# An attention and feed-forward kernel: the input weights kept resident in float32, their state product made plainly by row halves

## The chip, the cores and the metric

One Trainium2 chip, one core of it. The metric is the device time of one execution in microseconds (us); lower is better. The kernel before took 725.33, 726.32 and 727.12 us in three runs, median 726.32. Differences below about 0.3% can't be told from no change.

## The reference

```
scores  = x @ state^T / sqrt(D);  a  = softmax(scores);   xread = a @ state     # (B, H, S, D)
scores2 = state @ x^T / sqrt(D);  a2 = softmax(scores2);  sread = a2 @ x        # (B, H, N, D)
X = concat([xread, sread], rows)          # B*(S+N) = 8*(512+32) rows of H*D = 512
h = X @ w_in;  r = max(h, 0);  out = (r * r) @ w_out       # w_in 512x2048, w_out 2048x512
```

B = 8 batches, H = 8 heads, S = 512, N = 32 states, D = 64. x and state come as float32, the two weight matrices as float64, and the kernel turns them into float32 by integer work on their 64-bit words.

## The kernel before

The rows of xread never exist: since xread @ w_in = a @ (state @ w_in), the kernel makes z = state @ w_in once for each half of the batches (G = 0 and 1, four batches each), and then `ph` = z^T a for 512 rows of a batch and 128 columns of w_in at a time. Nearly every product is made of "high" and "low" parts (a float32 value is split by `split` into a rounded float32r copy, by ACT, and the rest, by DVE or POOL), three matmuls for one product.

**Units.** The main work is 128 units, 16 for each batch, one for each slice `fc` of 128 of the 2048 columns. A unit has an "up" (six matmuls into `ph`, line 394), then relu, square and split on ACT and DVE (lines 396 to 404), and a "down" (twelve matmuls into four accumulators `po`, line 420). A pair of units shares one z tile, numbered k = fc // 2. `BOTH` lists the first stretches of units: batch 0 with fc 0 to 5, batch 1 with 0 to 9, batch 0 with 6 to 15, batch 1 with 10 to 15; then batches 2 to 7 whole. Below, units are numbered 0 to 127 in that order.

**Weights.** w_in comes as 16 tiles of 512 KB (`w_raw`), w_out as 16 (`wo_raw`). Both go through the four buffers of tag `raw`. `singles` turns one into float32 (one ACT instruction, line 107, and four on DVE, lines 108, 109, 113 and 117). w_out is then split and stays on the chip (`wo_hi`, `wo_lo`; the low part by POOL). w_in is written as float32 to DRAM (`wd`, line 165), for the z work of the second half and for the last stage to read again (lines 156 and 626).

**z.** `z_part` makes the z of one w_in tile: two products, one for each 64-row half of the operands (head 2q + i lies in rows 64i to 64i + 63). The first six tiles of G = 0 are plain float32 (line 192), the others use split operands (line 204; 12 matmuls a tile in G = 0, 8 in G = 1). Results go over ACT (line 216) to DRAM (`zd`), and `z_fetch` reads the 128 rows that a batch needs back (line 230) and splits them.

**Attention.** For each batch and each of two head groups: `xt_raw` is split, `pq` matmuls give scores (line 291), then a softmax chain (lines 296 to 330) leaves `a_hi` and `a_lo` for the ups; the other direction is turned (line 345) and read out (line 357). `a_hi` and `a_lo` have two buffers, so a batch's pair comes free when the batch two before it is done.

**Order.** The program emits steps by due times (class `Ahead`); a scheduler then decides the order on each engine from the emitted priority and its own view of when data is there. Each engine runs its list strictly in order. SP issues the loads and the output stores, ACT the `zd` stores.

**Last stage.** The 256 rows of sread of all batches go through 16 further units of half the size (line 642), with w_in read again from `wd`.

## Time and profile before

| | |
|---|---|
| median of three runs | 726.32 us |
| span of the profiled execution, first to last instruction | 721.4 us |
| PE busy (matmuls, 3152) | 670.0 us, 93% |
| DVE busy | 470.8 us, 65% |
| ACT busy | 393.5 us, 55% |
| POOL busy | 200.5 us, 28% |
| moved by DMA | 90.52 MB, mean 125 GB/s |

The profile gives the execution's span and not a time of its own; the median of the runs lies 4.9 us above the span. Shares over the whole span hide that the kernel has stages: a first one of about 145 us in which the weights are turned to float32, a long one of even units, and the last stage from 666 us. The rows that carry the argument stand in the prediction. In them a group of instructions has its line, engine, operation, out<-in names, shapes, count, then busy time and the mean in ns of one instruction, then the idle time before it and what ended it. Matmul records overlap, so starts of neighbours, not their durations, tell what one costs.

### The profile page before, as it was taken

How to read it: one execution, taken by the hardware profiler on the slowest of the kernel's cores; microseconds unless marked ns; L12 is line 12 of the kernel's file. 1: busy time of each engine (PE TensorE's matmuls, PEld its weight loads, DVE VectorE, ACT ScalarE, POOL GpSimd, SP SyncE). 2: the span in 40 equal slices, each digit the busy share in tenths (PEclk: the TensorE clock that was granted, in tenths of full speed). 3: DMA queues.
4: the chain of work that ended last, by engine and by line, in shares of the span. 5: the costliest groups of instructions: out<-in, count | busy, mean ns of one | idle time of the engine just before them, and what ended most of it. 6: DMA issues, size and time to landing. Idle time of an engine off the chain costs nothing.

```text
span 721.4 us, 9309 instructions
## 1 busy us (share of the span) xinstructions
PE 670.0 (93%) x3152; PEld 551.7 (76%) x3152; DVE 470.8 (65%) x789; ACT 393.5 (55%) x711; POOL 200.5 (28%) x181
## 2 busy tenths in 40 slices
PE   4577779999999999999999999999999999999994
PEld 2345567788888888888888878878888888888893
DVE  6869998968456964456945883897754436443551
ACT  3557686587555774466735554666554335332441
POOL 3313342354541551053404232333332022000000
PEclk9689899999999999999999999999999999999998
DMA  9787778744253452243323212422141112100320
GB/s 320 239 263 241 261 261 268 214 137 137 94 172 115 150 166 96 87 134 131 124 84 122 82 53 66 141 78 90 58 146 66 33 35 80 37 1 27 120 59 30
DMA packets 72436, 90.52 MB, mean 125 GB/s; under 512 B 3781, under 2 KB 55749, under 8 KB 72389
## 3 DMA queue, kind: packets, MB, share of 16 engines
q1 hardware_dynamic: 54980, 73.15, 31.4%
q10 hardware_dynamic: 17408, 16.78, 6.9%
q8 instruction: 25, 0.41, 0.2%
q14 instruction: 23, 0.18, 0.1%
HBM read 60.03 MB, written 29.88 MB: 125 GB/s over the span
## 4 chain that ended last, share of the span: by engine, by line
PE 72%; DVE 17%; DMA 4%; ACT 3%; issue 3%; SPq 0%; POOL 0%; DVEq 0%; ACTq 0%; POOLq 0%
PE po L420 43%; PE ph L394 23%; PE pr L357 2%; DMA wo_raw<-w_out 2%; PE pz L204 2%; DVE wf L113 2%; DMA z_raw<-zd 1%; DVE sp_hl L252 1%; DVE z_lo L98 1%; DVE g_lo L98 1%; DVE wof L113 1%; PE pq L291 1%; PE pt L345 1%; DVE wf L117 1%; DVE wf L108 1%
## 5 line engine op out<-in xcount | busy, mean ns | idle before, releaser
L420 PE MATMUL po<-wo_hi,g_hi 128*128 128x512 f32 x544 | 217.4, 401 | 3.0 <-ACT g_hi L97 2.9
L420 PE MATMUL po<-wo_lo,g_hi 128*128 128x512 f32 x544 | 213.1, 393 | 0.0
L400 DVE TENSOR_TENSOR ph<-ph,r 128x512 f32<-128x512 f32 (+1 forms) x134 | 89.0, 664 | 161.9 <-ACT r L396 161.8
L396 ACT ACTIVATE r<-ph 128x512 f32<-128x512 f32 (+1 forms) x144 | 82.2, 573 | 165.2 <-PE ph L394 164.6
L420 PE MATMUL po<-wo_hi,g_lo 128*128 128x512 f32 x544 | 151.3, 390 | 2.4 <-DVE g_lo L98 2.4
L420 PEld LDWEIGHTS po<-wo_hi,g_hi 128*128 128x128 f32 x544 | 103.3, 190 | 26.3 <-ACT g_hi L97 4.9
L98 DVE TENSOR_TENSOR g_lo<-ph,g_hi 128x512 fp32r<-128x512 f32 (+1 forms) x144 | 94.4, 655 | 40.7 <-ACT g_hi L97 30.4
L420 PEld LDWEIGHTS po<-wo_hi,g_lo 128*128 128x128 f32 x544 | 101.0, 188 | 23.3 <-DVE g_lo L98 3.2
L420 PEld LDWEIGHTS po<-wo_lo,g_hi 128*128 128x128 f32 x544 | 103.5, 190 | 19.7 <-issue 0.2
L97 ACT CAST g_hi<-ph 128x512 fp32r<-128x512 f32 (+1 forms) x144 | 81.1, 563 | 48.6 <-DVE ph L400 43.0
L394 PE MATMUL ph<-a_hi,z_hi 128*128 128x512 f32 x256 | 81.1, 398 | 2.7 <-DVE g_lo L98 1.6
L394 PE MATMUL ph<-a_hi,z_lo 128*128 128x512 f32 x256 | 79.3, 390 | 0.0
L394 PE MATMUL ph<-a_lo,z_hi 128*128 128x512 f32 x256 | 79.0, 390 | 0.0
L98 POOL TENSOR_TENSOR xn_hl<-xn_raw,xn_hl 128x1024 fp32r<-128x1024 f32 x16 | 39.5, 2471 | 131.2 <-issue 72.1
L183 POOL TENSOR_TENSOR w<-wf,w 64x512 fp32r<-64x512 f32 x32 | 42.1, 1315 | 64.0 <-ACT w L182 60.3
L394 PEld LDWEIGHTS ph<-a_hi,z_hi 128*128 128x128 f32 x256 | 47.2, 190 | 14.4 <-DVE g_lo L98 3.0
L394 PEld LDWEIGHTS ph<-a_hi,z_lo 128*128 128x128 f32 x256 | 48.1, 188 | 10.4
L394 PEld LDWEIGHTS ph<-a_lo,z_hi 128*128 128x128 f32 x256 | 48.0, 188 | 10.2
L98 POOL TENSOR_TENSOR xt_hl<-xt_raw,xt_hl 128x1024 fp32r<-128x1024 f32 x12 | 29.2, 2435 | 70.6 <-ACT xt_hl L97 41.8
L98 DVE TENSOR_TENSOR z_lo<-z_raw,z_hi 128x512 fp32r<-128x512 f32 x64 | 46.9, 733 | 2.5 <-ACT z_hi L97 2.5
L98 POOL TENSOR_TENSOR wo_lo<-wof,wo_hi 128x512 fp32r<-128x512 f32 x16 | 25.9, 1620 | 67.1 <-ACT wo_hi L97 67.1
L97 ACT CAST z_hi<-z_raw 128x512 fp32r<-128x512 f32 x64 | 39.4, 616 | 5.8 <-DMA z_raw<-zd 5.3
(98 smaller groups left out, 853.1 us busy)
## 6 DMA issues: line engine op xcount, KB each, us to landing
zd<-z_stage ACTq DMA_DIRECT2D x64, 256.0 KB
...
```

The lines of the kernel that those rows point to most:

```text
L97: nc.scalar.copy(out=hi, in_=src)
L98: eng_lo.tensor_sub(out=lo, in0=src, in1=hi.bitcast(F32))
L108: nc.vector.tensor_scalar_max(out_f, out_f, 2.0**-15)
L113: nc.vector.scalar_tensor_tensor(out=bits, in0=high, scalar=-0x40000000, in1=bits, op0=ALU.bitwise_and, op1=ALU.bitwise_or,)
L117: nc.vector.scalar_tensor_tensor(out=bits, in0=low, scalar=29, in1=bits, op0=ALU.logical_shift_right, op1=ALU.bitwise_or,)
L183: nc.gpsimd.tensor_sub(out=w[other], in0=wf[own], in1=w[own].bitcast(F32))
L204: nc.tensor.matmul(pz[:, q, :], lhsT=a[:, h, :], rhs=w, start=j == 0, stop=j == len(todo) - 1,)
L357: nc.tensor.matmul(pr[:, q].rearrange("p i c -> p (i c)"), lhsT=my["e"][:, t, q].rearrange("p i n -> p (i n)"), rhs=my["xn"][:, t, q].rear ...
L394: nc.tensor.matmul(ph, lhsT=w, rhs=v, start=i == 0, stop=i == len(todo) - 1)
L396: nc.scalar.activation(r, ph, AF.Relu)
L400: nc.vector.tensor_mul(out=ph, in0=ph, in1=r)
L420: nc.tensor.matmul(po[t], lhsT=g, rhs=w, start=i == 0 and j == 0, stop=i == last and j == 2)
```

## The change

w_in stays on the chip as float32 in one tile `wi`; it is never written out, so `wd`, its stores and its later loads are gone. The z work reads `wi` plainly in float32: four matmuls for a tile, two heads for each 64-row half, with no split of w_in or of the state; both halves share one `z_stage` and one `zd` store of 512 KB. For batch 0 and k below 3, z is made directly by `z_direct` (operand `sp_f`, the state of batch 0 in block form) into PSUM and split from there, without DRAM; the same z parts for batches 1 to 3 are made later. `singles` loses its maximum: the scale `GUARD` of the ACT instruction takes its place. The factor 1/sqrt(D) moves from the state into the exponentials (one more small ACT instruction a group). `sp_hl` is split by ACT and DVE. x is split in halves (`x_hl` tiles of half the size, still one buffer). The low part of `a` of batch 0 is made on DVE. `BOTH` becomes batch 0 with fc 0 to 5, all of batch 1, then batch 0 with 6 to 15; `LATE` (how many batches later the read-out comes) goes from 3 to 2. Output rows go through three buffers `os_` in place of a whole-batch tile; what batch 0 has after its first visit is stored to DRAM and loaded again for the second. A z fetch is four DMAs in place of one, a store of the last stage is four on two queues.

```diff
-    PLAIN_Z = 6
+    DIRECT = 3
     PLAIN_X = 2
-    BOTH = ((0, 6), (1, 10), (0, NFC), (1, NFC))
-    LATE = 3
+    BOTH = ((0, 6), (1, NFC), (0, NFC))
+    LATE = 2
+    XHL = 1
+    GUARD = 2.0**-112
...
-    wd = [dr.tile([P, NCC, FW], F32, name=f"wd_{k}") for k in range(NFCH)]
-    zd, st, z_first = {}, {}, []
+    wi = const.tile([P, NFCH, NCC, FW], F32, name="wi")
+    zd, st = {}, {}
...
-        nc.scalar.activation(out_f, high.bitcast(F32), AF.Abs)
-        nc.vector.tensor_scalar_max(out_f, out_f, 2.0**-15)
+        nc.scalar.activation(out_f, high.bitcast(F32), AF.Abs, scale=GUARD)
         nc.vector.tensor_scalar(
-            out=bits, in0=bits, scalar1=3, scalar2=0x3FFFFFF8,
-            op0=ALU.logical_shift_left, op1=ALU.bitwise_and,
+            out=bits, in0=bits, scalar1=3, scalar2=None, op0=ALU.logical_shift_left
         )
         nc.vector.scalar_tensor_tensor(
-            out=bits, in0=high, scalar=-0x40000000, in1=bits,
+            out=bits, in0=high, scalar=-0x80000000, in1=bits,
             op0=ALU.bitwise_and, op1=ALU.bitwise_or,
         )
...
+        raw = sb.tile([P, NCC, GB * N], F32, name="st_z", bufs=1)
+        src = stT.rearrange("d (c i b n) -> i d c b n", i=2, c=NCC, b=B)
+        for i in range(2):
...
+        st[G] = raw
...
-            if G:
-                box["wf"] = sb.tile([P, nq, FW], F32, name="wf", bufs=2)
-                nc.sync.dma_start(out=box["wf"], in_=wd[k][:, ccs, :])
-                return
...
-            wf = sb.tile([P, nq, FW], F32, name="wf", bufs=2)
-            singles(wf, box["raw"])
-            nc.sync.dma_start(out=wd[k][:, ccs, :], in_=wf)
-            box["wf"] = wf
-
-        plain = G == 0 and k * NG + g < PLAIN_Z
...
-            if G == 0:
-                split(w2[0], w2[1], wf, nc.vector)
-                return
-            for i, w in enumerate(w2):
-                own = slice(i * D, (i + 1) * D)
-                other = slice((1 - i) * D, (2 - i) * D)
-                nc.scalar.copy(out=w[own], in_=wf[own])
-                nc.gpsimd.tensor_sub(out=w[other], in0=wf[own], in1=w[own].bitcast(F32))
-
...
-                    if plain:
-                        nc.tensor.matmul(
-                            pz[:, q, :], lhsT=st["raw"][own, h, :], rhs=box["wf"][own, q, :],
-                            start=True, stop=True,
-                        )
-                        continue
-                    st_hi, st_lo = st[G]
-                    u, v = (w[:, q, :] for w in box["w2"])
-                    todo = ((st_lo, u), (st_hi, u), (st_hi, v))
-                    if G:
-                        w = box["w2"][i][:, q, :]
-                        todo = (st_lo, w), (st_hi, w)
-                    for j, (a, w) in enumerate(todo):
-                        nc.tensor.matmul(
-                            pz[:, q, :], lhsT=a[:, h, :], rhs=w,
-                            start=j == 0, stop=j == len(todo) - 1,
-                        )
...
-                stage = sb.tile([P, nq, FW], F32, name="z_stage", bufs=3)
-                nc.scalar.copy(out=stage, in_=pz)
-                dst = zd[G, k].rearrange("p g (q i) f -> p g q i f", i=2)[:, g, :, i, :]
-                nc.scalar.dma_start(out=dst, in_=stage)
-            return run
-
...
-            raw = z_first[0]
-        else:
-            nc.sync.dma_start(out=raw, in_=zd[b // GB, k][at:at + N].rearrange("n g j f -> j n g f"))
+            singles(wi[:, k, g * nq:(g + 1) * nq, :], box.pop("raw"))
+
+        return load, convert
...
+    def z_part(G, k, g):
+        nq = NCC // NG
+
+        def product():
+            pz = [ps_x.tile([P, nq, FW], F32, name=f"pz{i}", tag="px") for i in range(2)]
+            for q in range(nq):
+                for i in range(2):
+                    own = slice(i * D, (i + 1) * D)
+                    cc = g * nq + q
+                    nc.tensor.matmul(
+                        pz[i][:, q, :], lhsT=st[G][own, cc, :], rhs=wi[own, k, cc, :],
+                        start=True, stop=True,
+                    )
+            stage = sb.tile([P, nq, 2, FW], F32, name="z_stage", bufs=2)
+            for i in range(2):
+                nc.scalar.copy(out=stage[:, :, i, :], in_=pz[i])
+            nc.scalar.dma_start(
+                out=zd[G, k][:, g].rearrange("p h f -> p (h f)"),
+                in_=stage.rearrange("p q i f -> p (q i f)"),
+            )
+
+        return product
+
+    def z_direct(k, pool, tag):
+        pz = pool.tile([P, NG, FW], F32, name="pzd", tag=tag)
+        nq = NCC // NG
+        for g in range(NG):
+            for q in range(nq):
+                nc.tensor.matmul(
+                    pz[:, g, :], lhsT=sp_f[:, g].rearrange("p q n -> p (q n)")[:, q * P:(q + 1) * P],
+                    rhs=wi[:, k, g * nq + q, :], start=q == 0, stop=q == nq - 1,
+                )
         hi = sb.tile([P, NG, FW], F32R, name="z_hi", bufs=2)
         lo = sb.tile([P, NG, FW], F32R, name="z_lo", bufs=2)
+        split(hi, lo, pz, nc.vector)
...
+        for j in range(HG):
+            nc.sync.dma_start(out=raw[j * N:(j + 1) * N], in_=src[:, :, j, :])
         split(hi, lo, raw, nc.vector)
...
             pair.extend(sb.tile([P, NG, S], F32R, name=n, bufs=2) for n in ("a_hi", "a_lo"))
+            src = stP[b].rearrange("p (g q n) -> p g q n", g=NG, q=2)
+            if b == 0:
+                for i in range(2):
+                    rows = slice(i * D, (i + 1) * D)
+                    nc.sync.dma_start(out=sp_f[rows, :, :, i * N:(i + 1) * N], in_=src[rows])
+                return
...
+            my["xt"] = []
+            for q in range(NQ):
+                hl = sb.tile([P, 2, S], F32R, name="xt_hl", tag="x_hl", bufs=XHL)
+                split(hl[:, 0], hl[:, 1], my["t"][:, q, :], nc.gpsimd)
+                my["xt"].append((hl[:, 0], hl[:, 1]))
...
+            nc.scalar.mul(nm2, nm2, SCALE)
...
-            nc.scalar.activation(e2, pst, AF.Exp, bias=nm2, accum_out=s2)
+            nc.scalar.activation(e2, pst, AF.Exp, bias=nm2, scale=SCALE, accum_out=s2)
...
-            split(pair[0][:, g, :], pair[1][:, g, :], at, nc.gpsimd)
+            split(pair[0][:, g, :], pair[1][:, g, :], at, pool_early(b))
...
+            for q in range(NQ):
+                hl = sb.tile([P, NT, 2, P], F32R, name="xn_hl", tag="x_hl", bufs=XHL)
+                split(hl[:, :, 0, :], hl[:, :, 1, :], raw[:, :, q, :], nc.gpsimd)
+                my["xn"].append(hl)
...
+    direct = {}
+
+    def z_now(k):
+        direct[k] = z_direct(k, ps_o, "po") if k < 2 else z_direct(k, ps_x, "px")
...
+        k = (m + 2) // NG
+        if (m + 2) % NG and k < DIRECT:
+            steps.append(lambda k=k: z_now(k))
+        if m >= DIRECT * NG:
+            steps.append(z0[m])
         weights.add(steps, 2 * min(at[m], at[m - m % FPC] - 2))
+        if m >= DIRECT * NG - 1:
+            for j in range(DIRECT * NG) if m == DIRECT * NG - 1 else ():
+                weights.add([z0[j]], 2 * (begins[1] - 3 + j // 2))
...
-                zc[k] = z_fetch(b, k)
+                zc[k] = direct.pop(k) if b == 0 and k < DIRECT else z_fetch(b, k)
...
-            if fcs[0] == 0:
-                if t == 0:
-                    sums[b] = sb.tile([P, NT, DM], F32, name="sum", bufs=2)
-                move(t, sums[b][:, t, :], po)
+            dst = sb.tile([P, DM], F32, name="os_", bufs=3)
+            if fcs[0]:
+                part = sb.tile([P, DM], F32, name="part", tag="raw", bufs=RAW)
+                nc.sync.dma_start(out=part, in_=spill[b, t])
+                nc.vector.tensor_add(out=dst, in0=part, in1=po)
             else:
-                nc.vector.tensor_add(out=sums[b][:, t, :], in0=sums[b][:, t, :], in1=po)
-            if fcs[-1] == NFC - 1:
-                nc.sync.dma_start(
-                    out=out[b * R + t * P:b * R + (t + 1) * P, :], in_=sums[b][:, t, :]
-                )
+                move(t, dst, po)
+            if fcs[-1] < NFC - 1:
+                spill[b, t] = dr.tile([P, DM], F32, name=f"part_{b}_{t}")
+                nc.sync.dma_start(out=spill[b, t], in_=dst)
+                return
+            nc.sync.dma_start(out=out[b * R + t * P:b * R + (t + 1) * P, :], in_=dst)
...
-        raw = sb.tile([P, NCC, P], F32, name="wi_raw", tag="raw", bufs=RAW)
-        nc.sync.dma_start(out=raw, in_=wd[k][:, :, i * P:(i + 1) * P])
-        w_hi = sb.tile([P, NCC, P], F32R, name="wi_hi", tag="w2_0", bufs=2)
-        w_lo = sb.tile([P, NCC, P], F32R, name="wi_lo", tag="w2_1", bufs=2)
-        split(w_hi, w_lo, raw, nc.vector)
+        w_hi = sb.tile([P, NCC, P], F32R, name="wi_hi", tag="z_hi", bufs=2)
+        w_lo = sb.tile([P, NCC, P], F32R, name="wi_lo", tag="z_lo", bufs=2)
+        split(w_hi, w_lo, wi[:, k, :, i * P:(i + 1) * P], nc.vector)
...
-        dst = out.rearrange("(b r) e -> b r e", r=R)[t * GB:(t + 1) * GB, S:R, :]
-        nc.sync.dma_start(out=dst, in_=tile_)
+        for j in range(GB):
+            at = (t * GB + j) * R + S
+            eng = nc.sync if j % 2 else nc.scalar
+            eng.dma_start(out=out[at:at + N, :], in_=tile_[j * N:(j + 1) * N, :])
```

How the scheduler laid the two programs out, at three places. First DVE, around the first unit of batch 1 (unit 6), before. `wof` and `wf` are w_out and w_in tiles on their way to float32; a unit's down waits for its `g_lo`:

```order
L113 SCALAR_TENSOR_TENSOR wof_763<-wo_raw_761,wof_763 128x512
L117 SCALAR_TENSOR_TENSOR wof_763<-wo_raw_761,wof_763 128x512
L98 TENSOR_TENSOR w2_1_990<-wf_890,w2_0_989 128x512
L98 TENSOR_TENSOR g_lo_758<-ph_741,g_hi_757 128x512
L108 TENSOR_SCALAR wf_1007<-wf_1007 128x512
L109 TENSOR_SCALAR wf_1007<-wf_1007 128x512
L98 TENSOR_TENSOR g_lo_808<-ph_797,g_hi_807 128x512
L113 SCALAR_TENSOR_TENSOR wf_1007<-w_raw_818,wf_1007 128x512
L108 TENSOR_SCALAR wof_822<-wof_822 128x512
```

Nine of the sixteen w_out tiles are converted ahead of unit 6's `g_lo_758`, and the others follow between later units. DVE at the same unit after the change:

```order
L112 SCALAR_TENSOR_TENSOR wof_1052<-wo_raw_1050,wof_1052 128x512
L105 TENSOR_SCALAR wof_1108<-wof_1108 128x512
L108 SCALAR_TENSOR_TENSOR wof_1108<-wo_raw_1104,wof_1108 128x512
L112 SCALAR_TENSOR_TENSOR wof_1108<-wo_raw_1104,wof_1108 128x512
L105 TENSOR_SCALAR wof_1153<-wof_1153 128x512
L108 SCALAR_TENSOR_TENSOR wof_1153<-wo_raw_1151,wof_1153 128x512
L112 SCALAR_TENSOR_TENSOR wof_1153<-wo_raw_1151,wof_1153 128x512
L99 TENSOR_TENSOR z_lo_806<-z_raw_807,z_hi_805 128x512
L99 TENSOR_TENSOR g_lo_670<-ph_650,g_hi_669 128x512
L99 TENSOR_TENSOR g_lo_705<-ph_694,g_hi_704 128x512
L99 TENSOR_TENSOR g_lo_734<-ph_714,g_hi_733 128x512
```

All sixteen w_out tiles, and all of w_in, now stand ahead of unit 6's `g_lo_670`; `wof_1153` is the last of them.

Second ACT, at the same unit, before. `g_hi_757` is the first operand of unit 6's down:

```order
L97 CAST wo_hi3_530<-wof_632 128x512
L216 COPY z_stage_944<-pz_937 128x512
L398 ACTIVATE ph_741<-r_754 128x512
L216 COPY z_stage_974<-pz_967 128x512
L398 ACTIVATE ph_797<-r_804 128x512
L97 CAST w2_0_989<-wf_890 128x512
L218 DMA zd_0_5_96<-z_stage_944 128x2x256
L97 CAST g_hi_757<-ph_741 128x512
```

It stands behind the split of the eighth w_out tile (`wo_hi3`). ACT at the same unit after the change, where the operand is `g_hi_669`:

```order
L355 ACTIVATE r_666<-ph_650 128x512
L355 ACTIVATE r_701<-ph_694 128x512
L98 CAST z_hi_805<-z_raw_807 128x512
L357 ACTIVATE ph_650<-r_666 128x512
L98 CAST wo_hi7_1106<-wof_1153 128x512
L157 COPY z_stage_856<-pz0_850 128x2x256
L357 ACTIVATE ph_694<-r_701 128x512
L157 COPY z_stage_856<-pz1_851 128x2x256
L98 CAST g_hi_669<-ph_650 128x512
L98 CAST g_hi_704<-ph_694 128x512
```

It now stands behind `wo_hi7_1106<-wof_1153`, the split of the last w_out tile, and behind two copies of z parts.

Third PE, at the first up of batch 3 (unit 48), before. `pt` and `pr` are the read-out of an older batch; `a_hi` and `a_lo` are what the softmax chain leaves:

```order
L394 MATMUL ph_2785<-a_hi_2196,z_hi_2788 128x512 x2
L394 MATMUL ph_2785<-a_hi_2196,z_lo_2789 128x512 x2
L394 MATMUL ph_2785<-a_lo_2197,z_hi_2788 128x512 x2
L345 MATMUL pt_2849<-ident_72,e2_476 128x128
L204 MATMUL pz_2881<-w2_0_2840,stz_lo_1949 128x256
L420 MATMUL po0_2071<-wo_hi7_1383,g_hi_2728 128x512
L420 MATMUL po0_2071<-wo_lo7_1384,g_hi_2728 128x512
```

No score matmul stands near; the last scores of batch 3 (`pq_2389`) come 236 rows earlier. PE at the first up of batch 3 after the change:

```order
L379 MATMUL po3_1977<-wo_hi7_1106,g_lo_2613 128x512
L353 MATMUL ph_2664<-a_hi_2113,z_hi_2665 128x512
L353 MATMUL ph_2695<-a_hi_2113,z_hi_2665 128x512
L247 MATMUL pq_2338<-xt_hl_2306,sp_hl_77 128x512
L151 MATMUL pz0_2375<-wi_83,st_z_1856 128x256 x2
L247 MATMUL pq_2338<-xt_hl_2306,sp_hl_77 128x512
L151 MATMUL pz1_2376<-wi_83,st_z_1856 128x256 x2
L304 MATMUL pt_2712<-ident_72,e2_1777 128x128 x4
L316 MATMUL pr_2745<-xn_hl_2689,e_hl_2717 128x256 x4
L304 MATMUL pt_2801<-ident_72,e2_1808 128x128 x4
L316 MATMUL pr_2745<-xn_hl_2692,e_hl_2717 128x256 x4
L353 MATMUL ph_2664<-a_hi_2113,z_hi_2665 128x512
```

The second half of `pq_2338`, the last scores of batch 3, now stands six rows ahead of the up that needs the result of its chain. Batch 2 begins in the same way.

More of the change, by code (lines that the diff above doesn't have):

```diff
@@ L233, in z_fetch @@
+    def z_fetch(b, k):
+        hi = sb.tile([P, NG, FW], F32R, name="z_hi", bufs=2)
+        lo = sb.tile([P, NG, FW], F32R, name="z_lo", bufs=2)
+        raw = sb.tile([P, NG, FW], F32, name="z_raw", bufs=2)
+        at = (b % GB) * N
+        src = zd[b // GB, k][at:at + N]
+        for j in range(HG):
+            nc.sync.dma_start(out=raw[j * N:(j + 1) * N], in_=src[:, :, j, :])
         split(hi, lo, raw, nc.vector)
@@ L448, in wo_load @@
         )
+        if i == 0:
+            wo[k] = [const.tile([P, FPC, DM], F32R, name=f"{n}{k}") for n in ("wo_hi", "wo_lo")]
         wf = sb.tile([P, DM], F32, name="wof", bufs=2)
         singles(wf, raw)
-        if i == 0:
-            wo[k] = [const.tile([P, FPC, DM], F32R, name=f"{n}{k}") for n in ("wo_hi", "wo_lo")]
         split(wo[k][0][:, i, :], wo[k][1][:, i, :], wf, nc.gpsimd)
@@ L574, in aux @@
         slot[0] += 1
-    sums = {}
+    spill = {}
     for b, fcs in parts:
```

111 lines of the change are left out of this document (25 added, 86 removed).

## The prediction

> **What bounds the kernel now.** I read the stretches first, to see where PE is short of work: busy time (and count) of PE, PEld, DVE, ACT, POOL, then PE's granted clock, the DMA engines' share, GB/s.
>
> ```profile
> core 0: us, PE busy (x) PEld busy (x) DVE busy (x) ACT busy (x) POOL busy (x), PEclk, DMA share, GB/s
> 8.00:60.00 52.00, 32.50 (x111) 20.95 (x110) 42.90 (x82) 30.46 (x60) 13.68 (x10) 0.80 0.84 275
> 60.00:145.00 85.00, 71.34 (x324) 57.81 (x325) 82.67 (x134) 56.07 (x105) 30.21 (x19) 0.92 0.76 245
> 145.00:666.00 521.00, 518.89 (x2439) 432.01 (x2438) 320.93 (x525) 285.02 (x498) 152.76 (x140) 1.00 0.29 94
> ```
>
> From 145 us on PE is the bound. Ahead of that DVE is: it is busy 82.67 of 85 us, and PE has gaps. The waits of PE from 145 us to the end are short:
>
> ```profile
> PE po L420 <- ACT g_hi L97: 2.1, 4, 0.8
> PE ph L394 <- DVE g_lo L98: 0.6, 1, 0.6
> ```
>
> How much PE has done by 145 us, from its groups in the first 145 us (two `a_hi,z_hi` matmuls an up, four `g_lo` matmuls a down):
>
> ```profile
> L420 PE MATMUL po<-wo_hi,g_lo 128*128 128x512 f32 x52 | 14.2, 394 | 2.4 <-DVE g_lo L98 2.4
> L394 PE MATMUL ph<-a_hi,z_hi 128*128 128x512 f32 x32 | 11.1, 432 | 2.1 <-ACT z_hi L97 1.1 <-DVE g_lo L98 1.0
> ```
>
> So 16 ups are done, and 13 downs; the fourteenth ends at 146.1 us. What a unit costs when nothing waits, from the chain of waits:
>
> ```profile
> 274.69 0.47 PE pz L204 x4
> ...
> 275.86 1.37 PE ph L394 x6
> 277.23 2.72 PE po L420 x12
> ```
>
> An up 1.37, a down 2.72, a split z matmul 0.47 / 4 = 0.117 us. The weights' conversion on DVE ends, in order of time, with the first row here; the others say what one conversion step takes alone (0.42), and beside a POOL instruction (1.26, 1.41, 1.51: the first, a middle one and the last of some 20 DVE records over 1.1 us):
>
> ```profile
> 144.07 0.69 DVE L117 SCALAR_TENSOR_TENSOR wof<-wo_raw,wof 128x512 int32<-128x512 int32 x1
> ...
> 12.26 1.26 DVE L109 TENSOR_SCALAR wf<-wf 128x512 int32<-128x512 int32 x1
> ...
> 135.97 0.42 DVE L108 TENSOR_SCALAR wof<-wof 128x512 f32<-128x512 f32 x1
> 136.42 1.41 DVE L109 TENSOR_SCALAR wof<-wof 128x512 int32<-128x512 int32 x1
> ...
> 140.40 1.51 DVE L108 TENSOR_SCALAR wof<-wof 128x512 f32<-128x512 f32 x1
> ...
> 136.19 1.36 POOL L98 TENSOR_TENSOR wo_lo<-wof,wo_hi 128x512 fp32r<-128x512 f32 x1 [2.02 <-ACT wo_hi L97]
> ```
>
> Before, then, the weights are ready at 144.8 us, and by then PE has worked off 14 units beside them.
>
> **The change, part by part.** The removed and moved DVE work of the first 145 us:
>
> ```profile
> L98 DVE TENSOR_TENSOR g_lo<-ph,g_hi 128x512 fp32r<-128x512 f32 x14 | 9.5, 678 | 0.9 <-ACT g_hi L97 0.9
> L108 DVE TENSOR_SCALAR wf<-wf 128x512 f32<-128x512 f32 x16 | 9.3, 584 | 3.8 <-ACT wf L107 3.8
> L108 DVE TENSOR_SCALAR wof<-wof 128x512 f32<-128x512 f32 x16 | 9.0, 565 | 4.7 <-ACT wof L107 4.7
> L98 DVE TENSOR_TENSOR z_lo<-z_raw,z_hi 128x512 fp32r<-128x512 f32 x9 | 7.2, 797 | 2.5 <-ACT z_hi L97 2.5
> L98 DVE TENSOR_TENSOR w<-wf,w 128x512 fp32r<-128x512 f32 x10 | 7.0, 699 | 0.0
> L400 DVE TENSOR_TENSOR ph<-ph,r 128x512 f32<-128x512 f32 x5 | 3.5, 691 | 0.0
> ```
>
> *End of the weights.* The DVE order of the change puts every conversion ahead of unit 6's `g_lo`, so I add up what DVE does until then. Busy before, to 145 us: 42.90 + 82.67 and about 1 ahead of 8 us, 126.7. Out go the maximum (9.3 + 9.0), the split of w_in (7.0), 8 of 14 `g_lo` (5.4), 5 `ph` (3.5) and 3 of 9 `z_lo` (2.4): 36.6. In come two `a_lo` of batch 0 at the price of a `g_lo`, 1.4. That leaves 91.5. If the maxima were worth only 0.42 each, since POOL's instructions then land on other steps, 32 x 0.42 = 13.4 go in place of 18.3, which leaves 96.4. I take 94. DVE starts at about 8 us: before, the first conversion began at 7.27, and now both 512 KB x loads are queued ahead of the first weight.
>
> ```profile
> 7.27 0.43 DVE L108 TENSOR_SCALAR wf<-wf 128x512 f32<-128x512 f32 x1 [2.29 <-ACT wf L107]
> ```
>
> To that come DVE's waits. Before, they were 52 - 42.90 = 9.1 us between 8 and 60, and 2.3 to 145. The `wd` stores no longer stand in SP's way, but loads must now keep pace with a faster DVE through the same four buffers. By count of the issues, about 27.7 MB must move by then (weights 16.8, x 3.1, `zd` stores 5.2, fetches and the rest 2.6); at 275 GB/s, the rate of 8 to 60 us, that is 101 us, at 235 GB/s 118. I take 8 us of waits: weights done at 8 + 94 + 8 = **110 us**; bounds 8 + 91.5 + 0 = 99.5, and 118 + 4 for the last tile, 122.
>
> *From there to unit 6's first down.* ACT's order has, behind the last conversion, its split, two copies of z parts, a square and `g_hi_669`: five instructions of about 0.6 us, and 0.5 for hand-overs: 3.5.
>
> ```profile
> L216 ACT COPY z_stage<-pz 128x512 f32<-128x512 f32 x35 | 20.5, 585 | 3.0 <-PE pz L204 2.8
> ```
>
> So at 113.5 us PE stands in front of down 6, with ups 0 to 7 done; before it stood at 146.1 us in front of down 14, with ups 0 to 15 done. That is the heart of it: 33 us earlier, 8 units behind.
>
> *The rest of PE's work.* Before it took 721.4 - 146.1 = 575.3 us. Added: 8 x (1.37 + 2.72) = 32.7. The z work changes: before, 134 matmuls (the counts of line 204 after 145 us) at 0.117, 15.7. After, two 64-row products a tile. Their price, from the plain tiles of before, in the stream of downs at full clock:
>
> ```profile
> 44.87 1.13 PE L192 MATMUL pz<-wf,st_f 64*128 64x256 f32 x4
> 45.93 1.20 PE L420 MATMUL po<-wo_hi,g_hi 128*128 128x512 f32 x4
> ...
> 48.90 1.14 PE L192 MATMUL pz<-wf,st_f 64*128 64x256 f32 x8
> ```
>
> One product of two matmuls (x4 records) holds PE from 44.80 to 45.93, 1.12 us. Two of different halves back to back (x8) take 1.14: they run beside each other. In the new order of G = 1, ten products stand alone (11.2), six pairs stand together (7.0), and three clusters of three or four last 2.0 each: 24.2; the last four tiles of G = 0 come to 5.7. Together 29.9, so +14.2, between +8 (all paired, 20 x 1.16 = 23.2) and +29 (none beside another, 40 x 1.12 = 44.8). Rest: 575.3 + 32.7 + 14.2 = **622.2**.
>
> The Trainium skill (TensorEngine Tiling (Array Packing), Key Properties) says that tiles operate independently but that switching the tiling mode drains TensorE. The x8 row bears out the first half; the second would be part of the 1.12 us that the row already holds, and nothing is added for it.
>
> *New waits.* Batches 2 and 3 begin right behind their last scores. The chain from there to `a_hi` runs through these:
>
> ```profile
> L296 ACT COPY st_low<-pq 64x512 f32<-64x512 f32 x24 | 13.4, 583 | 3.9 <-PE pq L291 3.5
> L297 DVE TENSOR_TENSOR st<-pq,st_low 64x512 f32<-64x512 f32 x24 | 16.3, 679 | 0.6 <-ACT st_low L296 0.2
> L306 DVE STREAM_TRANSPOSE q<-st 128x512 f32<-128x512 f32 x12 | 8.4, 700 | 0.2
> L317 DVE TENSOR_REDUCE m<-q 128x16 f32<-128x512 f32 x12 | 8.1, 672 | 0.0
> L318 DVE TENSOR_TENSOR q<-q,m 128x512 f32<-128x512 f32 x10 | 8.2, 815 | 0.0
> L319 ACT ACTIVATE q<-q 128x512 f32<-128x512 f32 x12 | 7.6, 632 | 2.4 <-DVE q L318 2.3
> L324 DVE TENSOR_REDUCE s<-q 128x16 f32<-128x512 f32 x12 | 8.1, 675 | 0.9 <-ACT q L319 0.9
> L327 DVE TENSOR_TENSOR q<-q,s 128x512 f32<-128x512 f32 x10 | 9.0, 903 | 0.2
> L329 DVE STREAM_TRANSPOSE at<-q 128x512 f32<-128x512 f32 x12 | 8.5, 707 | 1.5 <-POOL q L327 1.3
> L97 ACT CAST a_hi<-at 128x512 fp32r<-128x512 f32 x12 | 7.2, 618 | 11.8 <-DVE at L329 9.5 <-PE ph L394 2.2
> ```
>
> 7.0 us, and at least half a us for small steps left out. For batch 3, PE has about 2.6 us of other work between (one product 1.1, eight read-out matmuls, transposes), so some 5 us are lost; for batch 2 about 5.2 (seven products in clusters), so some 3. I take 8, between 0 (the scores come earlier than their place suggests, since PE waited elsewhere) and 14.
>
> *At nothing:* the 16 `nm2` instructions on ACT (busy 285 of 521 us), the halved x tiles (same elements), four DMA issues a fetch (they are ahead by a unit or more; each late fetch would cost a us). The three `os_` buffers make the fourth move of a batch wait for the first store; the next batch's ups and six downs cover it, and if not, a us or two at nine places. The last stage keeps its matmuls; its loads were hidden.
>
> **Sum.** 113.5 + 622.2 + 8 = 743.7 us of span, against 721.4. The profiled execution is given by its span; the median, 726.32, lies 4.9 above, so the time is **748.6 us**, 3.1% slower. Without the new waits it is 740.6.
>
> **Rivals.**
> 1. *DVE runs through and wins (faster).* POOL's instructions stretch DVE's: the 20 records over 1.1 us are each about 1 longer than alone (1.41 against 0.42). If half of that goes with the removed steps, and loads never wait, DVE is busy 84 and done at 92; no new waits: 92 + 3.5 + 622.2 = 717.7, time 722.6. It decides from an end of the weights of 95.7 downwards. For it: DVE sat idle only 2.3 of 85 us. Against: the same w_out splits on POOL remain, and 27.7 MB by 92 us would be 300 GB/s throughout. The Trainium skill (SBUF — State Buffer, Who interferes with whom) has DVE and GpSimd block each other for whole instructions; the 1.41 beside 0.42 agrees, and it is why I leave the lock's cost in. Chance 0.10, and 0.07 more that it only breaks even (724 to 728.5).
> 2. *Loads set the end of the weights.* At 235 GB/s, 122 us: 125.5 + 622.2 + 8 = 755.7, time 760.6. For it: four buffers are all that can be in flight, and a faster DVE gives each load less time. Against: DMA was at 0.84 and not full. Chance 0.17.
> 3. *The halves do not overlap* in the stream of split matmuls, since each clears the array. +15 over the sum: 763.5. Against: the x8 row. Chance 0.06.
> 4. *The new waits at batches 2 and 3 do not come,* and the weights end at 104: 107.5 + 622.2 = 729.7, time 734.6. Chance 0.15.
>
> **Numbers.** The forecast, 737 to 757, has 0.45. Range 726 to 764: below it lies nearly all of rival 1, above it the worst of 2 and 3. Faster by over 0.3% (what a measurement of this kernel can tell from no change) 0.11, within 0.3% 0.07, slower 0.82.
>
> **What would show it.** The last `wof` of DVE at about 110 us (rival 1: under 96; rival 2: about 122, with ACT's line 104 waiting for loads); the first down of unit 6 within 4 us of it; PE with few gaps from there to the last stage except about 3 and 5 us at the starts of batches 2 and 3; `pz` records of two halves that start together. The forecast is wrong if PE's stretch from down 6 to the end is not near 630 us.

## The result, and the profile after

The changed kernel takes **761.69 us** (median of four runs, 761.07 to 762.43); the kernel before, beside it, 726.02 us (725.33 to 727.12). The ratio is 1.0484, 95% interval [1.0463, 1.0505]: slower by 4.8%. The prediction was 748.6 us, with a range of 726 to 764. The profiled execution took 761.69 us over a span of 759.9.

| | before | after |
|---|---|---|
| span of the profiled execution | 721.4 us | 759.9 us |
| last w_out tile converted on DVE | 144.8 us | 107.4 us |
| first matmul of unit 6's down | 104.3 us | 111.7 us |
| first matmul of unit 14's down | 147.2 us | 150.6 us |
| from the first matmul of down 31 to that of down 32 | 4.8 us | 27.3 us |
| from down 47 to down 48, likewise | 5.4 us | 23.8 us |
| last unit's down ended | 666.3 us | 712.4 us |
| from there to the end | 55.1 us | 47.5 us |
| moved by DMA | 90.52 MB | 79.00 MB |

First the stretches of the changed kernel, with the columns of the prediction's first view. They are cut at unit 6's first down (111.65), at the starts of batches 2 and 3 (230.90 to 255.00 and 336.80 to 357.60, each from the last matmul of the batch before to the first down of the new one) and at the last stage (712.40).

```profile
core 0: us, PE busy (x) PEld busy (x) DVE busy (x) ACT busy (x) POOL busy (x), PEclk, DMA share, GB/s
8.00:60.00 52.00, 45.64 (x133) 27.94 (x134) 50.32 (x94) 32.60 (x64) 16.95 (x13) 0.80 0.77 252
60.00:111.65 51.65, 36.97 (x125) 24.06 (x123) 42.86 (x65) 33.59 (x63) 19.58 (x15) 0.81 0.79 275
111.65:230.90 119.25, 118.50 (x521) 93.99 (x520) 51.45 (x79) 51.03 (x92) 14.01 (x17) 0.98 0.24 80
230.90:255.00 24.10, 21.06 (x74) 13.99 (x74) 12.09 (x23) 14.01 (x30) 9.10 (x8) 0.79 0.43 166
255.00:336.80 81.80, 81.80 (x368) 62.13 (x368) 34.91 (x56) 39.26 (x71) 10.09 (x14) 1.00 0.32 112
336.80:357.60 20.80, 12.45 (x43) 8.81 (x41) 12.52 (x22) 11.00 (x23) 6.77 (x9) 0.67 0.31 116
357.60:712.40 354.80, 354.80 (x1606) 292.28 (x1607) 213.15 (x351) 176.37 (x329) 73.52 (x89) 1.00 0.20 65
712.40:759.90 47.50, 42.42 (x276) 38.11 (x274) 21.85 (x45) 18.95 (x45) 0.00 (x0) 0.98 0.10 34
```

Three things are to be seen. The weights' stretch is over early, though in its second half DVE is no longer full (42.86 of 51.65). In the long stretches PE is almost without a gap and at full clock. Between them lie two stretches of 24.1 and 20.8 us, with a granted clock of 0.79 and 0.67, in which PE does the work of two ups and a few small products. Before, the clock was 1.00 from 145 to 666 us in one piece.

What stands between the weights and unit 6's first down, from the timelines of ACT, PE and DVE in order of time:

```profile
97.98 0.62 ACT L98 CAST a_hi<-at 128x512 fp32r<-128x512 f32 x1
...
99.58 0.80 PE L353 MATMUL ph<-a_hi,z_hi 128*128 128x512 f32 x1
...
106.75 0.69 DVE L112 SCALAR_TENSOR_TENSOR wof<-wo_raw,wof 128x512 int32<-128x512 int32 x1
...
109.49 0.59 ACT L98 CAST g_hi<-ph 128x512 fp32r<-128x512 f32 x1
...
111.65 0.79 PE L379 MATMUL po<-wo_hi,g_hi 128*128 128x512 f32 x1
```

The last conversion ends at 107.44, `g_hi` is the fifth ACT instruction behind it, the down at 111.65: the prediction's 110 and 113.5 are met within 2.6 us. The first two rows have something that the prediction passed over. Batch 1's second `a_hi` is cast only at 97.98, and unit 6's up starts behind it.

The start of batch 2, from the timeline of all engines. It is the chain from the last score matmul to the first up that needs it:

```profile
231.87 0.50 PE L247 MATMUL pq<-xt_hl,sp_hl 128*128 128x512 f32 x1
...
232.59 0.58 ACT L252 COPY st_low<-pq 64x512 f32<-64x512 f32 x1
...
233.87 0.69 DVE L253 TENSOR_TENSOR st<-pq,st_low 64x512 f32<-64x512 f32 x1
...
235.53 0.71 DVE L262 STREAM_TRANSPOSE q<-st 128x512 f32<-128x512 f32 x1
...
236.73 0.68 DVE L274 TENSOR_REDUCE m<-q 128x16 f32<-128x512 f32 x1
237.48 1.05 POOL L275 TENSOR_TENSOR q<-q,m 128x512 f32<-128x512 f32 x1 [2.45 <-DVE m L274]
...
238.76 0.63 ACT L276 ACTIVATE q<-q 128x512 f32<-128x512 f32 x1
...
239.49 0.68 DVE L281 TENSOR_REDUCE s<-q 128x16 f32<-128x512 f32 x1
...
240.81 1.05 POOL L284 TENSOR_TENSOR q<-q,s 128x512 f32<-128x512 f32 x1 [2.28 <-DVE s L283]
...
241.89 0.71 DVE L286 STREAM_TRANSPOSE at<-q 128x512 f32<-128x512 f32 x1 [1.23 <-POOL q L284]
...
243.26 0.62 ACT L98 CAST a_hi<-at 128x512 fp32r<-128x512 f32 x1
...
245.39 0.63 PE L353 MATMUL ph<-a_hi,z_hi 128*128 128x512 f32 x1
```

The prediction priced this chain at 7.0 us. It takes 11.4 to the cast of `a_hi` (231.87 to 243.26) and 13.5 to the up. Most of the instructions are as long as in its rows; the two on POOL take 1.05 us each, where it had taken DVE rows of 0.82 and 0.90. The rest is other work that stands in the queues between two links: on ACT copies of z parts, on DVE an output tile, `sp_hl` and a reduction of the other direction. And while PE waits, its clock falls (windows inside the two starts):

```profile
234.60:239.30 4.70, 2.94 (x16) 2.05 (x16) 3.97 (x9) 3.23 (x8) 1.48 (x2) 1.00 0.51 190
239.30:249.50 10.20, 10.20 (x27) 6.91 (x26) 2.01 (x5) 3.58 (x7) 3.62 (x3) 0.50 0.42 169
341.70:355.30 13.60, 8.05 (x25) 6.39 (x25) 9.25 (x17) 5.65 (x13) 5.55 (x8) 0.50 0.23 83
```

At 0.50 it stays for 10.2 and for 13.6 us, over the very matmuls that end the wait. The longest single gap between two matmul starts ahead of the first fall is 1.62 us. The Trainium skill (TensorE: Matmul & The Clock Gate, Part 1: The HAM clock gate) says that how busy PE has been in a window of about 3.4 us sets its clock. The fall fits that: 2.94 us busy of 4.70, in short pieces, was too little here. The return does not: in the next 10.2 us the profile counts PE as busy throughout, and the clock stays at 0.50.

How much is lost there: the two steps take 51.0 us, 40.8 more than before. In them stand seven z tiles (56 matmul records, 8.1 us at the 1.16 of a pair, 15 if every half paid 1.06 alone), 20 read-out, 12 transpose and 4 score matmuls (some 4 us) and one up more each (2.7). That leaves about **26 us of waiting and half clock (19 if every half paid alone), where the prediction had 8**.

### The profile page after: what moved, and what is told of

Its sections match the earlier page's. It is cut to its first block, busy times and chain, and to the rows that moved or that the text cites. A ratio compares the mean times of both kernels' runs of the same rounds, so it can differ in the third digit from the quotient of the medians.

```text
span 759.9 us, 9457 instructions
## 1 busy us (share of the span) xinstructions
PE 713.6 (94%) x3136; PEld 561.3 (74%) x3136; DVE 439.1 (58%) x729; ACT 378.3 (50%) x714; POOL 151.9 (20%) x170
## 4 chain that ended last, share of the span: by engine, by line
PE 82%; DVE 9%; DMA 4%; ACT 2%; issue 2%; POOL 0%; SPq 0%; DVEq 0%; ACTq 0%; POOLq 0%
PE po L379 47%; PE ph L353 25%; PE pz L151 4%; PE pr L316 2%; PE pst L257 1%; PE pq L247 1%; DMA w_raw<-w_in 1%; DVE wof L112 1%; DVE wof L108 1%; DVE wi L108 1%; DMA part<-os__634 1%; PE pt L304 1%; DVE wi L112 1%; DMA part<-os__646 1%; DMA sp_f<-stP 1%
## 5 line engine op out<-in xcount | busy, mean ns | idle before, releaser
L379 PE MATMUL po<-wo_lo,g_hi 128*128 128x512 f32 x544 | 215.9, 397 | 0.0
L99 POOL TENSOR_TENSOR xn_hl<-xn_raw,xn_hl 128x512 fp32r<-128x512 f32 x32 | 42.3, 1321 | 223.6 <-ACT xn_hl L98 223.6
L353 PE MATMUL ph<-a_hi,z_hi 128*128 128x512 f32 x256 | 85.4, 412 | 0.8 <-ACT a_hi L98 0.7
L353 PE MATMUL ph<-a_hi,z_lo 128*128 128x512 f32 x256 | 84.1, 411 | 0.0
L353 PE MATMUL ph<-a_lo,z_hi 128*128 128x512 f32 x256 | 82.7, 404 | 0.0
L151 PE MATMUL pz<-wi,st_z 64*128 64x256 f32 x256 | 63.2, 446 | 13.6 <-ACT z_stage L157 12.8
L151 PEld LDWEIGHTS pz<-wi,st_z 64*128 64x128 f32 x256 | 38.1, 207 | 37.0 <-ACT z_stage L157 18.8
L99 POOL TENSOR_TENSOR xt_hl<-xt_raw,xt_hl 128x512 fp32r<-128x512 f32 x24 | 31.5, 1312 | 161.7 <-ACT xt_hl L98 161.7
L353 PEld LDWEIGHTS ph<-a_hi,z_lo 128*128 128x128 f32 x256 | 50.9, 199 | 12.2 <-issue 0.7
L157 ACT COPY z_stage<-pz 128x512 f32<-128x512 f32 x64 | 36.5, 588 | 32.7 <-PE pz L151 30.1
```

The source lines that it names most:

```text
L99: eng_lo.tensor_sub(out=lo, in0=src, in1=hi.bitcast(F32))
L151: nc.tensor.matmul(pz[i][:, q, :], lhsT=st[G][own, cc, :], rhs=wi[own, k, cc, :], start=True, stop=True,)
L157: nc.scalar.copy(out=stage[:, :, i, :], in_=pz[i])
L353: nc.tensor.matmul(ph, lhsT=w, rhs=v, start=i == 0, stop=i == len(todo) - 1)
L379: nc.tensor.matmul(po[t], lhsT=g, rhs=w, start=i == 0 and j == 0, stop=i == last and j == 2)
```

## The experiments

First a summary. "Step" is the time from the first matmul of one down to that of the next; the ratio is to the kernel before, with its 95% interval.

| run | first down of unit 6 | step 31 to 32 | step 47 to 48 | median | ratio |
|---|---|---|---|---|---|
| before | 104.3 | 4.8 | 5.4 | 726 to 727 | 1 |
| after | 111.7 | 27.3 | 23.8 | 761.69 | 1.0484 [1.0463, 1.0505] |
| e1 early starts | 112.7 | 17.4 | 25.0 | 765.05 | 1.0533 [1.0504, 1.0562] |
| e2 old visits | 112.5 | 38.8 | 30.1 | 781.93 | 1.0767 [1.0715, 1.0819] |
| e3 order alone, in before | 105.9 | 6.3 | 6.8 | 733.24 | 1.0085 [1.0053, 1.0116] |
| e4 conversion alone, in before | 104.0 | 4.8 | 5.4 | 719.47 | 0.9887 [0.9848, 0.9926] |
| e5 z spread | 112.3 | 26.5 | 5.3 | 759.09 | 1.0460 [1.0437, 1.0483] |
| e6 LATE 3 | 117.3 | 6.4 | 27.8 | 762.98 | 1.0507 [1.0483, 1.0531] |
| e7 e5 and e6 | 118.5 | 4.9 | 8.6 | 753.77 | 1.0386 [1.0362, 1.0410] |
| e8 e7, batch 1 earlier | 96.8 | 4.9 | 8.6 | 743.11 | 1.0249 [1.0206, 1.0292] |
| e9 e8, halves paired | 95.3 | 4.7 | 8.9 | 758.07 | 1.0433 [1.0415, 1.0450] |
| e10 e4 and the tail, in before | 101.8 | 4.8 | 5.4 | 712.03 | 0.9798 [0.9783, 0.9813] |
| e11 less room, in before | 109.8 | 4.6 | 4.8 | 731.49 | 1.0069 [1.0048, 1.0091] |
| e12 e8, old visits | 99.7 | 5.5 | 9.4 | 743.23 | 1.0226 [1.0205, 1.0247] |

### Is it the order of the visits?

The first theory was that of the prediction: the order of the visits leaves more units behind the weights and lets batches 2 and 3 start behind their scores. **e1** gives batch 2 the attention buffers of batch 1, which come free at unit 22 and not at 32, and lets its steps begin from there, with an earlier due time. Batch 3 takes those of batch 0, free from unit 32; its steps stood behind those of batch 2 before, so for it little changes:

```diff
-            pair.extend(sb.tile([P, NG, S], F32R, name=n, bufs=2) for n in ("a_hi", "a_lo"))
+            own = b if b < 2 else (b + 1) % 2
+            pair.extend(
+                sb.tile([P, NG, S], F32R, name=n, tag=f"{n}{own}", bufs=1) for n in ("a_hi", "a_lo")
+            )
...
-            reads.add(steps, 2 * begins[b] - 1, 2 * ends[b - 2] if b > 1 else 0)
+            reads.add(steps, 2 * begins[b] - (11 if b == 2 else 1), 2 * ends[{2: 1, 3: 0}.get(b, b - 2)] if b > 1 else 0)
...
```

> The changed kernel, but batch 2's attention takes the a_hi and a_lo buffers of batch 1 (free from unit 22) and batch 3's those of batch 0 (free from unit 32), and batch 2's attention steps are due five units before its first unit. Theory A (PE stands at the starts of batches 2 and 3 behind their own late scores, 24.1 and 20.8 us for some 13 and 7 us of work, so about 25 us): about 740 us, and the step from the last down of one batch to the first of the next falls to 6 to 10 us at both places. Rival B (the z products in lone row halves and the halved x tiles are what costs, wherever the scores stand): 755 to 762 us. Under both the first down of unit 6 stays at 110 to 113 us.

Batch 2's step fell to 17.4 us, batch 3's stayed at 25.0, and the time was 765.05. So the earliest permitted step explains a part of batch 2's wait, and mending it gains no time. Of batch 3's wait e1 shows only that it does not hang on batch 2's.

**e2** puts the old visits into the changed kernel, **e3** the new ones into the kernel before:

```diff
-    BOTH = ((0, 6), (1, NFC), (0, NFC))
+    BOTH = ((0, 6), (1, 10), (0, NFC), (1, NFC))
```

> The changed kernel with the four visits of before, (0,6),(1,10),(0,all),(1,all); all else as changed. Theory A (eight units fewer are left when the weights are ready, worth 33 us, and no late starts, worth some 25): about 705 us, below the kernel before, since its weights come earlier by more than 30 us; by the time of the last wof PE has done 14 units or more. Rival B (the new z, the halves of x and LATE of 2 cost what the order is blamed for): above 726 us.

> The kernel before with only the visits changed to (0,6),(1,all),(0,all). Theory A: eight units are left behind the weights (33 us), the weights themselves end no earlier than at 140 us, and batches 2 and 3 start behind their scores (10 to 25 us): 765 to 785 us. Rival B (order is harmless): 724 to 735 us.

Both went against the theory. With the old visits the changed kernel is 20 us slower still, its first down of unit 6 (112.5) and of unit 14 (150.4 against 150.6) where they were, and both starts worse. The new visits cost the kernel before 6 us, not 40. So in the changed kernel the visits do not set where PE stands when the weights are ready, and by themselves, in the kernel before, they make no start late. **e12**, further down, repeats the question where the starts are mended.

### What makes the scores late

In the changed kernel, the first half of batch 3's x is cast at 278 us, and its score matmuls run 26 us later (timeline):

```profile
278.41 0.62 ACT L98 CAST xt_hl<-xt_raw 128x512 fp32r<-128x512 f32 x1
...
304.38 0.63 PE L247 MATMUL pq<-xt_hl,sp_hl 128*128 128x512 f32 x2
```

Between them stand z parts of batches 4 to 7. There are sixteen, each takes both `ps_x` buffers, and the program may issue one in every slot from batch 2's first unit on, although their due times reach to the end of batch 3. Before, each z tile was four steps instead of one, and took four times as many slots. **e5** lets a part start two slots ahead of its due time:

```diff
-        weights.add([z1[m]], due, 2 * z1_from)
+        weights.add([z1[m]], due, due - 2)
```

> The changed kernel, but each z product of batches 4 to 7 may be issued only from two half-unit slots ahead of its own due time; before, all could be issued from batch 2's first unit, and were, one in each slot. Theory D (these sixteen parts, each taking both ps_x buffers, stand ahead of batch 3's scores in the ring of ps_x and in PE's queue): batch 3's scores move from its first unit to some ten units ahead, the step from down 47 to down 48 falls from 23.8 us to under 9, time 744 to 750 us. Rival (halves of x with one buffer make batch 3's scores late by themselves): the step stays over 18 us, time 757 to 763 us.

The mechanism is right and the gain is not. Batch 3's scores now run at 282 us, and its first down follows the last of batch 2 with no wait (timeline of PE):

```profile
281.85 0.63 PE L247 MATMUL pq<-xt_hl,sp_hl 128*128 128x512 f32 x2
...
332.42 0.62 PE L353 MATMUL ph<-a_hi,z_hi 128*128 128x512 f32 x2
332.88 0.62 PE L353 MATMUL ph<-a_hi,z_lo 128*128 128x512 f32 x2
333.33 0.62 PE L353 MATMUL ph<-a_lo,z_hi 128*128 128x512 f32 x2
333.88 1.13 PE L151 MATMUL pz<-wi,st_z 64*128 64x256 f32 x8
334.95 0.50 PE L379 MATMUL po<-wo_hi,g_hi 128*128 128x512 f32 x1
```

The step is 5.3 us, down from 23.8, and unit 50 comes 24 us earlier than in the changed kernel. But the time falls by 2.6 us only. The wait had held work, which now stands in the stream: batch 3 from unit 50 to 64 takes 76.0 us and not 63.2 (six z tiles more, 10.6 us of PE's order), and from unit 64 to 127 it takes 286.5 and not 278.3 (16 more read-out matmuls, 2 us, and short waits).

**e6** takes `LATE` back to 3, so that batch 0's read-out no longer goes through the one `x_hl` buffer ahead of batch 2's scores:

```diff
-    LATE = 2
+    LATE = 3
...
-            at = sb.tile([P, S], F32, name="at", bufs=2)
+            at = sb.tile([P, S], F32, name="at", bufs=1)
...
-            dst = sb.tile([P, DM], F32, name="os_", bufs=3)
+            dst = sb.tile([P, DM], F32, name="os_", bufs=2)
```

> The changed kernel with LATE back at 3 (the room comes from at with one buffer in place of two and os_ with two in place of three). Theory D (with LATE 2 the read-out of batch 0 goes through the one x_hl buffer ahead of the scores of batch 2): batch 2's scores move to unit 18 to 23, the step from down 31 to down 32 falls from 27 us to under 9; batch 3's start stays above 18 us; time 740 to 748 us. Rival (batch 2 is late because its steps may not begin before unit 32): the step at batch 2 stays over 18 us, time 757 us or more.

Batch 2's step fell to 6.4 us, though its steps still may not begin before unit 32, and batch 3's stayed long, at 27.8: the two starts have two causes, as expected. The time did not move. Unit 6 came 5.7 us later (117.3), and units 34 to 47 took 75.7 us in place of 68.9, with the work that had filled the wait.

**e7** has the edits of e5 and e6 together.

> The edits of e5 and e6 together. Theory D: both starts fall to under 9 us, together some 33 us of waits less the z work that now stands in the stream: 724 to 737 us. If the two edits only move the wait elsewhere: above 745 us.

Both steps are short, 4.9 and 8.6 us, and the time is 753.77: 8 us better than the changed kernel, not 25 to 38. Of the 51.0 us in the two steps 13.5 are left, but work comes back into the stream, and unit 6 comes 6.9 us later.

### What holds unit 6 back

**e8** moves batch 1's attention forward in e7:

```diff
-            reads.add(steps, 2 * begins[b] - 1, 2 * ends[b - 2] if b > 1 else 0)
+            reads.add(steps, 5 if b == 1 else 2 * begins[b] - 1, 2 * ends[b - 2] if b > 1 else 0)
```

> The kernel of e7 with batch 1's attention due three units earlier (slot 5 in place of 11). In the changed kernel batch 1's first a_hi came at 98 us, and unit 6's g_lo stands behind all 64 conversions on DVE; now it stands behind 58. If batch 1's attention is what holds unit 6 back: its first down at 98 to 106 us in place of 111.7, and the time 5 to 12 us under e7. If the weights are: the first down stays within 3 us of e7's, and so does the time.

```profile
71.30 0.61 ACT L98 CAST a_hi<-at 128x512 fp32r<-128x512 f32 x1
...
96.80 0.47 PE L379 MATMUL po<-wo_hi,g_hi 128*128 128x512 f32 x1 [0.88 <-ACT wof L104]
```

Batch 1's second `a_hi` is cast at 71.30 (97.98 in the changed kernel, 104.74 in e7), the first down of unit 6 starts at 96.80, almost ten us ahead of the weights' end (106.4), and the time falls by 10.7 us. Batch 1's attention held unit 6, not the weights. By unit 14 half of the 21.7 us is given back (146.3 against 156.6): z tiles that stood ahead of unit 6 now stand behind it, 60 `pz` records or 12.7 us of PE's order between units 6 and 14, in e7 16 records or 2.9 us.

**e12** gives e8 the old visits again.

> The kernel of e8 with the four visits of before, (0,6),(1,10),(0,all),(1,all). In e8 the weights end at 106.4 us and only two units' g_lo stand between conversions. If the visits as such matter (fewer units are left when the weights are ready): the first down of unit 14 comes 5 us or more ahead of e8's 146.3, time 730 to 738 us. If they do not, and e2 lost by the starts of batches 2 and 3 alone: unit 14 within 3 us of e8's, both starts under 9 us, time 740 to 748 us.

743.23 against 743.11 us: no difference, with both starts still short. Unit 14 comes 5.1 us earlier, as the first theory had it, and by unit 30 it is lost (221.5 against 221.0). So e2's loss fits its starts: its two steps are 17.9 us longer than those of the changed kernel, its span 23.0.

### What the plain z costs

In e8, behind the first down of unit 6, the `pz` matmuls take 47.5 us of PE's order (from each start to the next, 204 records), in before 24.7 (176 records). Most halves stand alone (timeline of PE in e8):

```profile
296.14 1.07 PE L379 MATMUL po<-wo_hi,g_lo 128*128 128x512 f32 x4
297.14 1.13 PE L151 MATMUL pz<-wi,st_z 64*128 64x256 f32 x4
298.20 0.73 PE L353 MATMUL ph<-a_hi,z_hi 128*128 128x512 f32 x2
...
299.23 0.40 PE L353 MATMUL ph<-a_lo,z_hi 128*128 128x512 f32 x1
299.56 1.13 PE L151 MATMUL pz<-wi,st_z 64*128 64x256 f32 x4
300.62 0.50 PE L353 MATMUL ph<-a_lo,z_hi 128*128 128x512 f32 x1
```

A lone half holds PE for 1.06 us; in e5, above, the x8 row with both halves of a tile holds it for 1.07. The tiles' busy time in two stretches of e8 says the same: 16 records, two tiles, in pairs; then 48 records, six tiles, apart.

```profile
146.30:182.20 35.90, 2.27 (x16) 1.38 (x16) 2.15 (x4) 1.00 0.33 114
240.10:309.00 68.90, 13.10 (x48) 7.65 (x48) 7.04 (x12) 1.00 0.29 96
```

1.13 us a tile together, 2.18 apart. **e9** ties the halves together:

```diff
...
+            nc.tensor.matmul(
+                pz[0][:, 0, :1], lhsT=st[G][:D, g * nq, :], rhs=wi[:D, k, g * nq, :1],
+                start=True, stop=True,
+            )
+            lead = half(0, 1)
+            with tc.issue_after(lead.ins):
+                for q, i in [(0, 0)] + [(q, i) for q in range(1, nq) for i in (1, 0)]:
+                    half(q, i)
...
```

> The kernel of e8 with the two row halves of each z product tied together on PE: a one-column matmul takes the first half's ps_x buffer, and the real matmuls follow only when the second buffer is there too. In e8 204 pz matmuls behind unit 6 cost 47.5 us of PE's order, 255 to 264 ns each where halves stand alone and 133 where they stand together. If lone halves are a main cost: some 130 to 180 ns each, 10 to 18 us off, time 725 to 734 us. Rival (the halves' price is the drain of each change of row mode, paired or not, or the pairs just hold both ps_x buffers longer): 740 us or more.

```profile
246.80:306.70 59.90, 4.38 (x30) 2.86 (x30) 3.23 (x6) 1.00 0.22 73
```

The price of a tile does fall (30 records, three tiles with their one-column matmuls: 1.46 us each in place of 2.18), but the time rises by 15 us to 758.07. Units 14 to 31 take 89.3 us against 78.8 in e8, units 50 to 64 88.1 against 75.3. In each of the two stretches stand eight score matmuls, which take 6.7 and 7.1 us of PE's order (2.4 and 2.0 in e8). That fits the second half of the expectation's rival, that a part which holds one buffer until it has the other keeps the scores out of `ps_x`; which waits come from that was not shown. In the later stretch the clock is 0.88 and a tile costs 1.90. Pairs that do not hold a buffer were not tried.

### Parts that pay

**e4** has the new conversion alone in the kernel before.

```diff
-        nc.scalar.activation(out_f, high.bitcast(F32), AF.Abs)
-        nc.vector.tensor_scalar_max(out_f, out_f, 2.0**-15)
+        nc.scalar.activation(out_f, high.bitcast(F32), AF.Abs, scale=GUARD)
...
```

> The kernel before with only the new conversion (no maximum on DVE, the guard in the scale of the ACT step). 32 DVE steps of 0.57 us go, 18.3 us of a DVE that is busy 82.67 of 85 us. Theory A (DVE is the bound to the end of the weights): weights end 13 to 18 us earlier, time 708 to 714 us. Rival C (POOL's instructions and the loads then stretch what is left): 718 to 725 us.

719.47 us, rival C's figure. 18.3 us of DVE work go, but the last conversion ends (at 134.99) only 9.8 us earlier than before. Most of the rest went into waits: between 8 and 135 us DVE waits 15.3 us for ACT's first step of a conversion (6.2 before), and ACT 20.2 us for loads of weights (11.5 before). So DVE was the bound until then, but the loads came close behind it. The last conversion:

```profile
134.31 0.68 DVE L112 SCALAR_TENSOR_TENSOR wof<-wo_raw,wof 128x512 int32<-128x512 int32 x1
```

**e10** adds the last stage's store in eight DMAs on two queues.

```diff
-        dst = out.rearrange("(b r) e -> b r e", r=R)[t * GB:(t + 1) * GB, S:R, :]
-        nc.sync.dma_start(out=dst, in_=tile_)
+        for j in range(GB):
+            at = (t * GB + j) * R + S
+            eng = nc.sync if j % 2 else nc.scalar
+            eng.dma_start(out=out[at:at + N, :], in_=tile_[j * N:(j + 1) * N, :])
```

> The kernel before with two of the change's parts alone: the new conversion (e4) and the last stage's output in eight DMAs on two queues in place of two DMAs on one. In the trace of before the last issue, at 712.3 us, is followed by 9 us to the end of the span; in the changed kernel by 3.6 us. If the store is what ends the span: 4 to 6 us under e4's 719.5, so 713 to 716 us. If that tail is launch overhead that no store sets: 718 to 721 us.

712.03 us, 0.9798 of the kernel before, and the best of all kernels here. From PE's last matmul to the end of the span it takes 5.2 us, in e4 10.3; the remaining 2 us came in the weights' stretch, and nothing in this edit explains them. e4's own four runs lie between 714.3 and 720.2.

**e11** makes the kernel before save the room that `wi` needs, and nothing else: `LATE` 2, and x in halves through one half-size buffer.

```diff
-    LATE = 3
+    LATE = 2
+    XHL = 1
...
-            hl = sb.tile([P, 2, NQ, S], F32R, name="xt_hl", tag="x_hl", bufs=1)
-            hi, lo = hl[:, 0], hl[:, 1]
-            split(hi, lo, my["t"], nc.gpsimd)
-            my["xt"] = hi, lo
+            my["xt"] = []
+            for q in range(NQ):
+                hl = sb.tile([P, 2, S], F32R, name="xt_hl", tag="x_half", bufs=XHL)
+                split(hl[:, 0], hl[:, 1], my["t"][:, q, :], nc.gpsimd)
+                my["xt"].append((hl[:, 0], hl[:, 1]))
...
```

> The kernel before with the two savings of memory alone: LATE 2 and the x tiles split in halves through one half-size buffer. If these by themselves make the scores of batches 2 and 3 late: the steps from down 31 to 32 and 47 to 48 grow from 4.8 and 5.4 us to over 12, time 740 us or more. If they need the z parts of the change in ps_x and the late batch 0 beside them: both steps stay under 8 us, time 724 to 732 us.

731.49 us, and both starts as short as before. The savings cost 5 us, and in the profiled run, the slowest of six (734.42), the loss stands ahead of unit 14 (its first down at 155.9 against 147.2) and not at the starts: late scores need the other parts of the change beside them.

## Why the prediction was right, and where not

The sign was right, and the time lies in the range, 2.3 us under its upper end. The forecast of 737 to 757, which had 0.45, was missed. The span came out 16.2 us above the sum (759.9 against 743.7), the time only 13.1 above (761.69 against 748.6), since the prediction put 4.9 us between span and median, and here it is 1.8. The profiled execution of before was a quick one: another run of it with a span of 721.7 us took 723.82. With 4.9 the measured span would have given 764.8, outside the range; that it holds is in part luck.

*End of the weights, 110 us; first down, 113.5:* right in size, 107.4 and 111.65. The reason was half right. DVE's order does put all conversions ahead of unit 6's `g_lo`, but they could only be put there because batch 1's attention was late; e8 moved it, and unit 6 went ahead of the weights' end.

*"33 us earlier, 8 units behind":* right as a sum, since it leaves unit 14 about where it was (the first matmul of its down at 150.6, 147.2 before). Wrong as a cause: e2 and e12 change the visits back, and unit 14 gains 0.2 and 5.1 us, and the run nothing. A part of what ate the earlier weights is that units 6 to 13 waited for batch 1's attention: from e7 to e8 unit 14 gains 10.3 us. Where the rest of the 37 us went was not shown; in e8, too, unit 14 comes only 0.9 us earlier than before. The ups and downs of units 6 to 13 took 36.0 us, 32.7 in the sum.

*Rest of PE's work, z at 29.9 us, +14.2:* not far off. From unit 6 on the `pz` matmuls take 36.4 us of PE's order, from each start to the next; but 18.5 of that stand in the two late starts, where PE waits or has half clock, and where the seven tiles would take 8.1 as pairs. With 8.1 for those it is 25.9, 4 under the sum. The other matmuls are the same in number.

*New waits, 8 us:* **this is the step that failed, by its size.** The place was right, both starts; the loss was about 26 us. The step counted the links of the chain at their lone durations and let PE's other work run beside them. It left out the foreign instructions between the links (11.4 us for 7.0) and the fall of the clock. It also took the place of the scores in PE's order as given by the visits. The runs show two other causes, each at one start: `LATE` 2 at batch 2 (e6; beside other parts of the change, since e11 has `LATE` 2 and no late start) and the z parts that all come at once at batch 3 (e5).

*The last stage at nothing:* wrong by 7.6, 47.5 us in place of 55.1. From PE's last matmul to the end it takes 5.1 us, 10.3 before, and e10 shows that the store's form, with its second queue, is worth that.

The balance of the span against the sum: -1.9 for the first down, +3.3 for units 6 to 13, +18 for the starts, -4 for z, -7.6 for the last stage; the remaining 8 us are spread over the stream and were not traced.

*Rivals.* 1 (DVE runs through) did not come: 107.4 and not 95.7. 2 (loads set the end) neither, though they were near: between 60 us and the last conversion ACT waited 7.8 us for loads of weights, and DVE 3.8 for ACT's first step. 3 (halves do not overlap) is wrong as put, since pairs take 1.07 us; but where the order sets halves apart, each pays in full. 4 (no new waits) is the opposite of what came.

*What stays open:* mending both starts (e7) brought 8 us, and an earlier batch 1 (e8) 11 more. Against before, e8's span of 740.9 is 19.5 longer: +22.8 from z behind unit 6 (its waits included), -7.5 from the earlier unit 6, -5 from the store; the +9 that are left were not traced. Whether z in pairs, without a held buffer, would bring it down to before was not shown.
